# A decode block with adaLN, sliding-window attention and an MLP: the tile framework replaced by a recorder in the kernel, and another end of the program

## Chip, cores and metric

One Trainium2 chip, one of its cores. The metric is the device time of one execution in microseconds, the median of several runs. All times below are from the chip.

## What is computed

Two tokens (B = 2, one position each, D = 512) pass through one block. A vector `c` gives six modulation vectors through SiLU and one matrix. Attention reads the last W = 4096 positions of a cache of 32768, with 32 query heads over 8 key/value heads of width 128. The MLP has F = 1792 hidden units. Everything is fp32.

```python
mod = (_silu(c) @ w_mod).reshape(c.shape[0], 6, 1, -1)
sa, ca, ga, sb, cb, gb = (mod[:, i] for i in range(6))
h = _layernorm(x) * (1 + ca) + sa
q = (h @ wq) as 32 heads
p = softmax(q @ k_cache[:, :, Sk - W:].T * Dh ** -0.5)   # 4 query heads share a kv head
x = x + ga * ((p @ v_cache[:, :, Sk - W:]) @ wo)
h = _layernorm(x) * (1 + cb) + sb
x = x + gb * (_silu(h @ w1) @ w2)
```

The inputs that are read: w_mod 6.3 MB, wq 8.4 MB, the windows of both caches 67 MB, wo 8.4 MB, w1 and w2 3.7 MB each; 97.5 MB in all. The result is 4 KB.

## The kernel before

The kernel is written in a framework (a tile context). The kernel asks for tiles from pools and calls engine operations; the framework orders the instructions of each engine, except where `inorder` pins them, and puts in the semaphores. It closes the program on leaving the context (line 569, inside `kernel`): SyncE waits for all semaphores, the engines meet, GpSimd clears the semaphores, the engines meet again. Line 558 is the constructor of the program object; it writes some constants and lets the engines meet once at the start.

**Memory.** One tile `store` of 36,864 floats on each of 128 partitions holds four slots of 8,192 floats (4 MB each) and a spare part. w_mod first lies in the last third, over slot 3 and the spare part; wq lies in slots 0 and 1.

**Loads.** SyncE issues all big loads, in this order: w_mod (line 78), wq in two halves (86), then K and V of eight steps (line 93, in `load_cache`) in the order k0, k1, v0, k2, v1, ..., k7, v6, v7, one slot each in rotation; then wo in four pieces, w1 in three and w2 in five (line 405, in `load_rows`). Each load waits until the engines have read what lay in its slot. ACT issues two small loads, c and x (line 82). `fetch` decides how far ahead the program text issues loads.

**Start.** GpSimd makes an identity matrix, and DVE sums pieces of it into small selection matrices (lines 107 to 139). `moments` (182 to 200) takes mean and variance of x with two small matmuls and a Sqrt on ACT. `silu_exp` (174 to 177) gives SiLU of c through an Exp on ACT. Matmuls with w_mod (222) give `m_a` (the first two modulation vectors) and `m_b` (the other four); `h_a` (230) is the modulated input. Matmuls with wq (242) give q, which is spread into `qbd` (253 to 267).

**Attention.** `seq` has eight steps: four pairs of kv heads, two tokens. A step t has three parts. `scores(t)` (287 to 322): four DVE transposes of the K slot, each followed by matmuls with `qbd`; then the row maximum, its spread over the partitions through two matmuls, and an Exp with row sums on ACT. `probabilities(t)` (327 to 345) turns the result for the next product. `values(t - 1)` (355 to 365): 16 matmuls over the V slot and, for the second token of a pair, four that collect `o_all`. The loop runs scores(t), values(t - 1), probabilities(t); these instructions are pinned in this order.

**End.** The sums of the softmax (`lp`, 424) are inverted and give the normalised output `oTn` (443). `product` and `narrow` (456) are the matmuls with wo, w1 and w2, some over 512 columns and some over 128. `fill` (451) issues matmuls that nobody reads. After wo come the residual, the second LayerNorm (482 to 506), w1, SiLU, and w2: products 0 to 7 into `yw`, copied by ACT (466) and folded by a matmul with `id4` into `y`, into which the last six products go as w2's last pieces land. DVE multiplies by gb and adds the residual (542, 543), and SyncE stores (545).

Of the kernel before, what the change touches and what calls it, by code (L numbers as in the profile page):

```python
# [1 line left out]

# [6 lines left out]
F32 = mybir.dt.float32  # L9
AF = mybir.ActivationFunctionType  # L10
ALU = mybir.AluOpType
AX = mybir.AxisListType

P = 128
# [11 lines left out]
@with_exitstack  # L26
def adaln_block(
    ctx: ExitStack,
    tc: tile.TileContext,
    x: bass.AP,  # L30
    k_cache: bass.AP,
    v_cache: bass.AP,
    wq: bass.AP,
    wo: bass.AP,
    w1: bass.AP,
    w2: bass.AP,
    c: bass.AP,
    w_mod: bass.AP,
    out: bass.AP,
):  # L40
# [6 lines left out]
    nc = tc.nc  # L47
# [6 lines left out]
    big = ctx.enter_context(tc.tile_pool(name="big", bufs=1))  # L54
    store = big.tile([P, 36864], F32, name="store")
    slot = [store[:, i * SLOT : (i + 1) * SLOT] for i in range(4)]
    consts = ctx.enter_context(tc.tile_pool(name="consts", bufs=1))
    ktp = ctx.enter_context(tc.tile_pool(name="ktp", bufs=3))
    work = ctx.enter_context(tc.tile_pool(name="work", bufs=2))
    once = ctx.enter_context(tc.tile_pool(name="once", bufs=1))  # L60
    psum = ctx.enter_context(tc.tile_pool(name="psum", bufs=2, space=bass.MemoryType.PSUM))
    psum1 = ctx.enter_context(tc.tile_pool(name="psum1", bufs=1, space=bass.MemoryType.PSUM))
    inorder = tc.keep_in_program_order

    def const(shape, name):
        return consts.tile(shape, F32, name=name)

    def bank(tag, name):
        return (psum1 if tag in "CO" else psum).tile([P, 512], F32, tag=tag, name=name)
# [4 lines left out]
    for t in (c_sp, x_sp):  # L74
        nc.vector.memset(t, 0.0)
    rows8 = lambda t: t.rearrange("(ab r) m -> ab r m", r=16)[:, 0, :]
    wm = store[:, 24576:36864].rearrange("p (k e) -> p k e", k=4)
    nc.sync.dma_start(
        wm.rearrange("p k e -> p (k e)"), w_mod.rearrange("(p k) e -> p (k e)", k=4)
    )  # L80
    for t, src in ((c_sp, c), (x_sp, x2)):
        nc.scalar.dma_start(rows8(t), src.rearrange("b (g m) -> g b m", m=P))
    wqt = store[:, :16384].rearrange("p (k e) -> p k e", k=4)
    wq4 = wq.rearrange("(p k) e -> p (k e)", k=4)
    for i in range(2):
        nc.sync.dma_start(slot[i], wq4[:, i * SLOT : (i + 1) * SLOT])
# [4 lines left out]
    def load_cache(cache, t, where):  # L91
        hp, b = seq[t]
        nc.sync.dma_start(
            where,
            cache[b, 2 * hp : 2 * hp + 2, SK - W :, :].rearrange(
                "u (i n) d -> i u (n d)", n=NK
            ),
        )
        return where
# [3 lines left out]
    make_identity(nc, ident)  # L103

    def summed(shape, name, pattern, axis=AX.X, **sizes):
        t = const(shape, name)
        nc.vector.tensor_reduce(t, ident.rearrange(pattern, **sizes), axis=axis, op=ALU.add)
        return t
# [3 lines left out]
    nc.vector.tensor_scalar(  # L112
# [3 lines left out]
    nc.vector.tensor_copy(  # L116
# [6 lines left out]
    nc.vector.tensor_reduce(  # L123
# [7 lines left out]
    nc.vector.tensor_reduce(  # L131
# [7 lines left out]
    nc.vector.tensor_reduce(  # L139
# [5 lines left out]
    for i in range(1, 4):  # L145
        nc.gpsimd.tensor_copy(pick[:, :, :, i], pick[:, :, :, 0])
        nc.gpsimd.tensor_copy(sums[:, :, :, i], sums[:, :, :, 0])
# [3 lines left out]
    nc.gpsimd.memset(mean512, 1.0 / D)  # L151
    negscale = const([1, 1], "negscale")
    nc.vector.memset(negscale, -SCALE)
    eps_t = const([P, 1], "eps_t")
    nc.vector.memset(eps_t, EPS)
    mrow = [const([1, P], f"mrow{i}") for i in range(2)]
    for t in mrow:
        nc.gpsimd.memset(t, 0.0)
    qbd = [const([P, 4, B, 4, 32], f"qbd{n}") for n in range(2)]
    qg = [const([P, 4, B, 4, G], f"qg{n}") for n in range(2)]  # L160
    for t in qg + qbd:
        nc.gpsimd.memset(t, 0.0)
    rowsum = const([P, NP], "rowsum")
    oTn = const([P, 32, 32], "oTn")
    nc.gpsimd.memset(oTn, 0.0)
# [3 lines left out]
    nc.gpsimd.memset(hT, 0.0)  # L169
    nc.gpsimd.memset(uT, 0.0)  # L170

    def silu_exp(t, name, shape):
        e = once.tile(shape, F32, tag="silu", name=name)
        nc.vector.tensor_scalar(e, t, -1.0, 87.0, op0=ALU.mult, op1=ALU.min)
        nc.scalar.activation(e, e, AF.Exp)
        nc.vector.tensor_scalar(e, e, 1.0, None, op0=ALU.add)
        nc.vector.reciprocal(e, e)
        return e

    def moments(t, name):  # L180
        st = work.tile([P, 6], F32, tag="st6", name=f"st_{name}")
        nc.vector.bn_stats(st, t)
        mv = work.tile([P, 2], F32, tag="mv", name=f"mv_{name}")
        nc.vector.bn_aggr(mv, st)
        avgm = avg.rearrange("p a r -> p (a r)")
        sm = bank("B", f"mean_{name}")
        nc.tensor.matmul(sm[:, 0:1], avgm, mv[:, 0:1], start=True, stop=True)  # L187
        mean = work.tile([P, 1], F32, tag="mean", name=f"m_{name}")
        nc.vector.tensor_copy(mean, sm[:, 0:1])
        dm = work.tile([P, 2], F32, tag="dm", name=f"dm_{name}")  # L190
        nc.vector.tensor_sub(dm[:, 0:1], mv[:, 0:1], mean)
        nc.vector.scalar_tensor_tensor(
            dm[:, 1:2], dm[:, 0:1], dm[:, 0:1], mv[:, 1:2], op0=ALU.mult, op1=ALU.add
        )
        sv = bank("B", f"var_{name}")
        nc.tensor.matmul(sv[:, 0:1], avgm, dm[:, 1:2], start=True, stop=True)
        std = work.tile([P, 1], F32, tag="std", name=f"sd_{name}")
        nc.scalar.activation(std, sv[:, 0:1], AF.Sqrt, bias=eps_t)
        rstd = work.tile([P, 1], F32, tag="rstd", name=f"rs_{name}")
        nc.vector.reciprocal(rstd, std)  # L200
        return mean, rstd

    def turned(t, name):
        o = const([P, 4, 32], name)
        nc.vector.transpose(o, t.rearrange("p (m k) -> p k m", k=4))
        return o
# [3 lines left out]
    xn = once.tile([P, P], F32, tag="xs", name="xn_a")  # L210
    nc.vector.tensor_scalar(xn, x_sp, mean_a, rstd_a, op0=ALU.subtract, op1=ALU.mult)
# [3 lines left out]
    nc.vector.tensor_mul(scT, cT, sg)  # L215
    m_a = bank("A", "m_a")[:, : 2 * P]
    m_b = bank("D", "m_b")
    for s0, s1, m in ((0, 2, m_a), (2, 6, m_b)):
        for k in range(4):
            v = wm[:, k].rearrange("p (s g m) -> p g s m", s=6, g=4)  # L220
            for g in range(4):
                nc.tensor.matmul(
# [6 lines left out]
    h_a = once.tile([P, P], F32, tag="h", name="h_a")  # L229
    nc.vector.scalar_tensor_tensor(h_a, m_a[:, P:], 1.0, xn, op0=ALU.add, op1=ALU.mult)  # L230
    nc.vector.tensor_add(h_a, h_a, m_a[:, :P])
    hq_T = turned(h_a, "hq_T")
    nc.scalar.copy(mod_sp[:, 2:, :].rearrange("p s m -> p (s m)"), m_b)
    nc.gpsimd.tensor_scalar(mod_sp[:, 4, :], mod_sp[:, 4, :], 1.0, None, op0=ALU.add)
    ga, sb, cb1, gb = (mod_sp[:, s, :] for s in range(2, 6))

    q_ps = [bank("D", f"q{n}") for n in range(2)]
    for k in range(4):
        for n in range(2):
            wv = wqt[:, k].rearrange("p (n s g m) -> p n g s m", n=2, s=4, g=G)  # L240
            for g in range(G):
                nc.tensor.matmul(  # L242
# [6 lines left out]
    for n in range(2):  # L249
        qT = once.tile([P, D], F32, tag="wide", name=f"qT{n}").rearrange(  # L250
            "p (s j r) -> p s j r", s=4, r=32
        )
        nc.vector.transpose(qT.rearrange("p s j r -> p (s j r)"), q_ps[n])  # L253
        for g in range(G):
            r = slice(32 * g, 32 * g + 32)
            eng = nc.gpsimd if g % 2 else nc.vector
# [3 lines left out]
        rp = bank("C", f"qr{n}")[:, :P]  # L260
        nc.tensor.matmul(
            rp, rep4, qg[n].rearrange("p s b j g -> p (s b j g)"), start=True, stop=True
        )
        for i in range(4):
            r = slice(32 * i, 32 * i + 32)
            cp = nc.scalar.copy if i % 2 else nc.vector.tensor_copy
# [12 lines left out]
    o_all = bank("O", "o_all")[:, : B * DH].rearrange("p (b d) -> p b d", b=B)  # L279

    def scores(t):
        hp, b = seq[t]
        s_ps = bank("A", f"s{t}")
        kv = kt[t].rearrange("p (n j r) -> p n j r", n=NK, j=4)
        for j in range(4):
            kT = ktp.tile([P, NK, 32], F32, tag="kT", name=f"kT{t}")
            inorder(nc.vector.transpose(kT, kv[:, :, j, :]))  # L287
            for u in range(2):
                h = 2 * hp + u
                for f in range(2):  # L290
                    r = 32 * (2 * u + f)
                    inorder(nc.tensor.matmul(  # L292
# [5 lines left out]
                    ))  # L298
        mx = work.tile([P, 1], F32, tag="mx", name=f"mx{t}")
        inorder(nc.vector.tensor_reduce(mx, s_ps, axis=AX.X, op=ALU.max))  # L300
        mT = bank("B", f"mT{t}")
        inorder(nc.tensor.matmul(mT[0:1, :P], mx, ident, start=True, stop=True))  # L302
        mg = work.tile([1, 2, G], F32, tag="mg", name=f"mg{t}")
        inorder(nc.vector.tensor_reduce(
# [6 lines left out]
        ))  # L311
        m = mrow[t % 2]
        for u in range(2):
            inorder(nc.vector.tensor_copy(  # L314
                m.rearrange("o (u f v a g) -> o u f v a g", u=2, f=2, v=2, g=G)[:, u, :, 0],
                mg[:, u, None, None, :].to_broadcast([1, 2, 4, G]),
            ))
        bp = bank("B", f"bp{t}")
        inorder(nc.tensor.matmul(bp[:, 0:1], m, negscale, start=True, stop=True))  # L319
        bias = work.tile([P, 1], F32, tag="bias", name=f"bias{t}")  # L320
        inorder(nc.scalar.copy(bias, bp[:, 0:1]))  # L321
        inorder(nc.scalar.activation(  # L322
            pr, s_ps, AF.Exp, bias=bias, scale=SCALE, accum_out=rowsum[:, t : t + 1]
        ))

    def probabilities(t):
        inorder(nc.vector.transpose(xp, pr))  # L327
        for f in range(2):
            inorder(nc.vector.tensor_mul(  # L329
# [3 lines left out]
            ))  # L333
        tp = bank("C", f"pT{t}")[:, : 4 * NK]
        for a in range(4):
            inorder(nc.tensor.matmul(  # L336
# [5 lines left out]
            ))  # L342
        pt = ptb[t % 2].rearrange("p (n u g) -> p n u g", u=2, g=G)
        for u in range(2):
            inorder(nc.scalar.activation(  # L345
                pt[:, :, u, :], tp.rearrange("p (n g) -> p n g", g=G), AF.Copy,
                scale=par[:, u : u + 1],
            ))

    def values(t):  # L350
        hp, b = seq[t]
        o_ps = bank("D", f"o{t}")
        for i in range(16):
            c_ = i % 4
            inorder(nc.tensor.matmul(  # L355
# [5 lines left out]
            ))  # L361
        inorder(nc.scalar.copy(ob[:, b].rearrange("p n d -> p (n d)"), o_ps))  # L362
        if b == B - 1:
            for n in range(4):
                inorder(nc.tensor.matmul(  # L365
# [6 lines left out]
                ))  # L372
# [29 lines left out]
    def load_rows(w, per, lo, hi, s, at):  # L402
        e = w.shape[1]
        n = (hi - lo) * e
        nc.sync.dma_start(s[:, at : at + n], w.rearrange("(p q) e -> p (q e)", q=per)[:, lo * e : hi * e])
# [13 lines left out]
    nc.vector.tensor_copy(hT[:, :, 1:32:16], sbT[:, :, 0:32:16])  # L419


    lp = bank("B", "lp")
    for hp in range(HP):
        nc.tensor.matmul(
# [6 lines left out]
    rl = once.tile([P, B], F32, tag="rl", name="rl")  # L431
    nc.vector.reciprocal(rl, lp[:, :B])
    rq = once.tile([P, B, 4], F32, tag="rq", name="rq")
    nc.vector.tensor_mul(
# [138 lines left out]
```

## Time and profile before

| | |
|---|---|
| median of 3 runs | 237.02 us (236.94 to 237.02) |
| the profiled execution | 237.04 us |
| its span, first to last instruction | 235.2 us |
| mean granted clock of TensorE | 0.832 |
| PE, DVE, ACT, POOL busy | 147.3, 113.2, 28.8, 7.1 us |
| moved by DMA | 97.68 MB, 415 GB/s over the span |

In profile lines PE is TensorE's matmul, PEld its weight load, DVE VectorE, ACT ScalarE, POOL GpSimd and SP SyncE; a "q" behind an engine (SPq) marks what its sequencer does: DMA issues, semaphore waits, drains. A timeline row has start, duration (both us), engine, line, operation, output <- inputs, shape and count; in square brackets, how long the engine stood idle before and what ended that. A row of stretches has the bounds, the length, the busy time of PE, PEld, DVE, ACT and POOL with instruction counts, TensorE's granted clock, the share of time in which the 16 DMA engines were busy, and GB/s. A row of DMA issues has the count, the size of each and the median time from issue to landing. A row of waits has the total, the number of waits and the longest. "instruction" queues carry the engines' own instructions.

### The profile page before, as it was taken

What the parts mean: (1) busy time and instruction counts of PE and PEld (TensorE: products, weight loads), DVE (VectorE), ACT (ScalarE), POOL (GpSimd) and SP (SyncE); (2) the same over time, 40 slices, a digit from 0 to 9 for tenths busy, and PEclk for the clock granted to TensorE, in tenths of its full rate; (3) what the DMA queues carried; (4) which work ended last, traced back from release to release, by engine and by line L of the source; (5) the groups of instructions that cost most, each with busy time, mean ns of one, the idle gap of its engine ahead of it and who ended that gap; (6) DMA issues with size and microseconds to landing.
All of it is one profiled execution on the core that took longest, in us unless ns stands there. A gap on an engine that the chain in (4) does not pass through costs nothing.

```text
span 235.2 us, 2446 instructions
## 1 busy us (share of the span) xinstructions
PE 147.3 (63%) x1024; PEld 39.8 (17%) x1024; DVE 113.2 (48%) x155; ACT 28.8 (12%) x64; POOL 7.1 (3%) x27
## 2 busy tenths in 40 slices
PE   0005953738258866887865838818757597677973
PEld 0003311110010211232101300200211132224212
DVE  0126110478397695894395387459439430102030
ACT  2010000010310120211200110210120102012210
POOL 5004000100000000000000000000000000000000
PEclk9999996756956797797679985976995759999799
DMA  7999999999999999999999999999999999999991
GB/s 267 461 432 429 418 426 418 446 440 446 425 429 412 426 446 435 440 426 418 423 440 429 437 440 423 423 429 437 435 430 429 429 426 440 401 415 418 421 400 41
DMA packets 4510, 97.68 MB, mean 415 GB/s; under 512 B 508, under 2 KB 532, under 8 KB 1044
## 3 DMA queue, kind: packets, MB, share of 16 engines
q1 hardware_dynamic: 4476, 97.52, 97.1%
q8 instruction: 8, 0.13, 0.2%
q14 instruction: 2, 0.02, 0.0%
q10 hardware_dynamic: 24, 0.01, 0.0%
HBM read 97.53 MB, written 0.00 MB: 415 GB/s over the span
## 4 chain that ended last, share of the span: by engine, by line
DMA 61%; DVE 23%; issue 6%; PE 6%; ACT 2%; SPq 0%; POOL 0%; POOLq 0%
DMA store<-in_A_k_cache_dram 25%; DVE kT L287 17%; DMA store<-in_A_wq_dram 16%; DMA store<-in_A_wo_dram 11%; DMA store<-in_B_w_dram 9%; PE q L242 2%; PE s L292 2%; DVE store L329 2%; ACT store L322 1%; DVE store L327 1%; DVE mx L300 1%; PE acc_y L456 1%; DVE qT L253 1%; ACT L322 1%; PE bp L319 1%
## 5 line engine op out<-in xcount | busy, mean ns | idle before, releaser
L287 DVE STREAM_TRANSPOSE kT<-store 128x2048 f32<-128x2048 f32 x32 | 71.1, 2280 | 15.8 <-DMA store<-in_A_k_cache_dram 15.7
L292 PE MATMUL s<-kT,qbd 128*32 128x512 f32 x256 | 49.5, 857 | 28.5 <-DVE kT L287 28.5
L355 PE MATMUL o<-store 128*32 128x512 f32 x256 | 38.2, 749 | 1.0 <-ACT store L345 1.0
L292 PEld LDWEIGHTS s<-kT,qbd 128*32 128x32 f32 x256 | 6.3, 126 | 66.4 <-DVE kT L287 65.7
L242 PE MATMUL q<-store,hq_T 128*32 128x512 f32 x64 | 9.7, 759 | 6.1 <-DMA store<-in_A_wq_dram 6.1
L355 PEld LDWEIGHTS o<-store 128*32 128x32 f32 x256 | 9.5, 132 | 22.4 <-issue 20.8
L187 PE MATMUL mean_a<-mv_a,avg 128*128 128x1 f32 x2 | 0.6, 362 | 18.8 <-DVE avg L112 18.8
L327 DVE STREAM_TRANSPOSE store<-store 128x512 f32<-128x512 f32 x8 | 5.7, 712 | 13.6 <-ACT store L322 13.6
L321 ACT COPY bias<-bp 128x1 f32<-128x1 f32 x8 | 1.3, 159 | 87.7 <-PE bp L319 87.7
L300 DVE TENSOR_REDUCE mx<-s 128x1 f32<-128x512 f32 x8 | 5.5, 692 | 11.0 <-PE s L292 11.0
L329 DVE TENSOR_TENSOR store<-store,half 128x512 f32<-128x512 f32 x16 | 10.4, 688 | 0.2
L336 PE MATMUL pT<-store,sel 128*32 128x256 f32 x64 | 7.5, 414 | 4.5 <-DVE store L329 4.5
L365 PE MATMUL o_all<-store,pick 128*32 128x256 f32 x32 | 7.7, 382 | 2.9 <-ACT store L362 2.9
L362 ACT COPY store<-o 128x512 f32<-128x512 f32 x8 | 4.7, 586 | 32.4 <-PE o L355 32.4
L345 ACT ACTIVATE store<-pT,par 128x256 f32<-128x256 f32 x16 | 6.7, 476 | 10.8 <-PE pT L336 10.8
L253 DVE STREAM_TRANSPOSE qT<-q 128x512 f32<-128x512 f32 x2 | 1.4, 717 | 13.3 <-PE q L242 13.0
L456 PE MATMUL acc_o<-store,oTn 128*32 128x512 f32 x48 | 5.6, 595 | 3.0 <-DMA store<-in_A_wo_dram 3.0
L302 PE MATMUL mT<-ident,mx 128*1 128x128 f32 x16 | 3.0, 271 | 6.5 <-DVE mx L300 6.5
L319 PE MATMUL bp<-negscale,mrow 1*128 1x1 f32 x16 | 3.2, 265 | 5.1 <-DVE mrow L314 5.1
L438 DVE TENSOR_TENSOR on<-o_all,rq 128x256 f32<-128x256 f32 x1 | 0.4, 425 | 12.2 <-PE o_all L365 12.2
L482 DVE STREAM_TRANSPOSE aoT<-ao 128x128 f32<-128x128 f32 x1 | 0.3, 317 | 11.6 <-PE ao L456 11.6
L451 PE MATMUL unread<-qbd,mean 128*128 128x256 f32 (+2 forms) x12 | 5.8, 566 | 0.1
(123 smaller groups left out, 93.4 us busy)
## 6 DMA issues: line engine op xcount, KB each, us to landing
store<-in_A_k_cache_dram SPq DMA_DIRECT2D x8, 4096.0 KB, 29.9
store<-in_A_v_cache_dram SPq DMA_DIRECT2D x8, 4096.0 KB, 29.8
store<-in_A_wq_dram SPq DMA_DIRECT2D x2, 4096.0 KB, 31.8
store<-in_w_mod_dram SPq DMA_DIRECT2D x1, 6144.0 KB, 17.2
store<-in_A_wo_dram SPq DMA_DIRECT2D x1, 4096.0 KB, 32.6
store<-in_B_w_dram SPq DMA_DIRECT2D x3, 1024.0 KB, 23.4
store<-in_A_wo_dram SPq DMA_DIRECT2D x1, 2048.0 KB, 25.1
store<-in_A_wo_dram SPq DMA_DIRECT2D x2, 1024.0 KB, 28.2
```

What stands on the lines that cost most here:

```text
L242: nc.tensor.matmul(q_ps[n][32 * g : 32 * g + 32, :], hq_T[:, k, :], wv[:, n, g], start=(k == 0), stop=(k == 3),)
L287: inorder(nc.vector.transpose(kT, kv[:, :, j, :]))
L292: inorder(nc.tensor.matmul(s_ps[r : r + 32, :], qbd[h // 4][:, h % 4, b, j, :], kT[:, 32 * f : 32 * f + 32, u:32:2], start=(j == 0), stop= ...
L300: inorder(nc.vector.tensor_reduce(mx, s_ps, axis=AX.X, op=ALU.max))
L327: inorder(nc.vector.transpose(xp, pr))
L329: inorder(nc.vector.tensor_mul(zp[:, 32 * f : 32 * f + 32, :].rearrange("p (s y) w -> p s y w", y=2), xp[:, :, None, 0:16].to_broadcast([P ...
L336: inorder(nc.tensor.matmul(tp[32 * a : 32 * a + 32, :], sel, zp[:, :, 4 * a : 4 * a + 4], start=True, stop=True,))
L345: inorder(nc.scalar.activation(pt[:, :, u, :], tp.rearrange("p (n g) -> p n g", g=G), AF.Copy, scale=par[:, u : u + 1],))
L355: inorder(nc.tensor.matmul(o_ps[32 * c_ : 32 * c_ + 32, :], ptb[t % 2][:, 32 * i : 32 * i + 32], vt[t][:, 512 * i : 512 * i + 512], start= ...
L365: inorder(nc.tensor.matmul(o_all[32 * hp : 32 * hp + 32, :, :], pick[:, n].rearrange("p w i -> p (w i)"), ob[:, :, n, :], start=(n == 0), ...
L451: inorder(nc.tensor.matmul(bank("C", "unread")[:, :n], mean512, idle_w[:, :n], start=True, stop=True))
L456: inorder(nc.tensor.matmul(acc[32 * g : 32 * g + 32, :n], w, rows, start=start, stop=stop))
```

## The change

The framework goes. `Flow` stands in its place: `fl.dve.tensor_mul(...)` and the like are recorded, not issued. For each operation `record` takes the region that it reads or writes of each tensor (first and last partition, first and last element in a partition, a box around strided accesses) and notes which earlier operations it must follow. `emit` then issues everything in program order. An operation waits for another engine's operation only where nothing that its engine has already waited for covers it. An engine other than TensorE also waits for its own earlier writes where they are read or overwritten; GpSimd waits for all its own earlier operations. Each engine has one semaphore, each DMA one of its own (34 of them).

At the end, the framework's closing is gone. PE, DVE, ACT and SyncE each add one to `done`, SyncE behind the issue of the store. GpSimd waits for the four and clears all semaphores but the store's. SyncE waits for the store and clears that one.

Pools become plain buffers: three for the transposed K pieces in turn (`kts`), two `wide` ones, eight PSUM banks handed out in turn by tag as before, and a buffer of its own for each small tile. The calculation, the shapes, the loads and the store are those of before. The text of the kernel body changes in names alone (`nc.vector` becomes `dve`, `inorder(...)` goes), but its order now is the order of every engine: the constants at the top, then `moments` of x, then SiLU of c; `lp` behind the last `values`.

The diff, cut to its core:

```diff
-    big = ctx.enter_context(tc.tile_pool(name="big", bufs=1))
-    store = big.tile([P, 36864], F32, name="store")
+    store = buf("store", P, 36864)
...
+class Flow:
+    NAMES = {"pe": "tensor", "dve": "vector", "act": "scalar", "pool": "gpsimd", "sp": "sync"}
...
+    def record(self, engine, method, args, kw):
+        aps = [(k, v) for k, v in (*enumerate(args), *kw.items()) if isinstance(v, bass.AP)]
+        outs = {0, "out", "accum_out"} if 0 in dict(aps) else {"out", "accum_out"}
+        me = len(self.ops)
+        needs = set()
+        for writes in (False, True):
+            for k, ap in aps:
+                if (k in outs) != writes or "dram" in ap.tensor.name:
+                    continue
+                r = self.region(ap)
+                held = self.seen.setdefault(ap.tensor.name, [])
+                for other, w, o in held:
+                    if (w or writes) and other != me and (
+                        r[0] < o[1] and o[0] < r[1] and r[2] < o[3] and o[2] < r[3]
+                    ):
+                        needs.add((other, w))
...
+        if engine == "pool":
+            needs |= {(i, True) for i, o in enumerate(self.ops) if o[0] == "pool"}
+        self.ops.append((engine, method, args, kw, needs))
+
+    def emit(self):
...
+        for i, (engine, method, _, _, needs) in enumerate(ops):
+            mine, wait = known[engine], []
+            for d, wrote in sorted(needs, reverse=True):
+                p = proc[d]
+                if p == engine and (engine == "pe" or not wrote):
+                    continue
+                if mine.get(p, -1) >= d:
+                    continue
+                wait.append(d)
+                told.add(d)
...
+            for d in waits[i]:
+                eng.wait_ge(*value[d])
+            ins = getattr(eng, method)(*args, **kw)
+            if method == "dma_start":
+                last = nc.alloc_semaphore(f"dma{i}")
+                ins.then_inc(last, 16)
+                value[i] = (last, 16)
+            elif i in told:
+                count[engine] += 1
+                ins.then_inc(sems[engine], 1)
+                value[i] = (sems[engine], count[engine])
+
+        for e in ("pe", "dve", "act", "sp"):
+            getattr(nc, self.NAMES[e]).sem_inc(done, 1)
+        nc.gpsimd.wait_ge(done, 4)
+        first = min(s.num for s in sems.values())
+        nc.gpsimd.sem_clear(range(first, last.num))
+        nc.sync.wait_ge(last, 16)
+        nc.sync.sem_clear(last)
...
-            inorder(nc.vector.transpose(kT, kv[:, :, j, :]))
+            kT = kts[(4 * t + j) % 3]
+            dve.transpose(kT, kv[:, :, j, :])
...
+    fl.emit()
...
-    with _tile.TileContext(nc) as tc:
-        adaln_block(tc, *args)
+    adaln_block(nc, *args)
```

404 lines of the change are left out of this document (215 added, 189 removed).

## The prediction

> **What bounds the kernel now.** I read the page first, then the stretches of the span, then the timeline of both ends, the instructions of the line that closes the program, and the DMA queue's own waits. From the page:
>
> ```profile
> span 235.2 us, 2446 instructions
> ...
> q1 hardware_dynamic: 4476, 97.52, 97.1%
> q8 instruction: 8, 0.13, 0.2%
> ...
> DMA 61%; DVE 23%; issue 6%; PE 6%; ACT 2%; SPq 0%; POOL 0%; POOLq 0%
> ```
>
> Queue q1 carries 97.52 MB and keeps the 16 DMA engines 97.1% busy: 228 of 235.2 us. The last line, the chain that ended last, tempts one to see 23% of DVE work that could shrink. The stretches, whose last columns are the granted clock, the DMA share and GB/s, say otherwise:
>
> ```profile
> 2.00:60.00 58.00, 26.58 (x168) 7.43 (x168) 20.60 (x44) 4.75 (x9) 5.72 (x17) 0.85 0.98 422
> 60.00:228.00 168.00, 117.93 (x796) 30.98 (x800) 91.65 (x106) 23.45 (x54) 0.00 (x0) 0.82 1.00 428
> 229.00:230.00 1.00, 0.42 (x8) 0.16 (x8) 0.00 (x0) 0.34 (x1) 0.00 (x0) 1.00 0.54 207
> 230.00:231.00 1.00, 0.95 (x36) 0.95 (x40) 0.00 (x0) 0.00 (x0) 0.00 (x0) 1.00 0.30 109
> ```
>
> From 60 to 228 us no DMA engine rests; only then do they finish, one after the other. The kernel is a stream of fixed length with a head and a tail, and only the head, the tail and what thins the stream can move the time. The profiled execution took 237.04 us, its span 235.2, so 1.8 us lie outside the span. The median of the runs is 237.02: what holds for this execution holds for it to 0.02 us.
>
> **The tail: what goes.** First the last steps of the timeline, then the instructions of line 569 up to 234.52 us, then those of the whole line (columns: engine, operation, count, shortest, median and longest in ns, first and last start):
>
> ```profile
> 230.05 1.70 PE L456 MATMUL acc_y<-store,uT 128*32 128x128 f32 x48 [0.23 <-DMA store<-in_B_w_dram]
> 231.31 0.16 PEld L456 LDWEIGHTS acc_y<-store,uT 128*32 128x32 f32 x8 [0.24 <-DMA store<-in_B_w_dram]
> 231.81 0.29 DVE L542 TENSOR_TENSOR yo<-acc_y,mod_sp 128x128 f32<-128x128 f32 x1 [5.33 <-PE acc_y L456]
> 232.13 0.29 DVE L543 TENSOR_TENSOR yo<-yo,x 128x128 f32<-128x128 f32 x1
> 232.45 0.69 SPq L545 DMA_DIRECT2D out_dram<-yo  x1
> ```
>
> ```profile
> L569 SPq EVENT_SEMAPHORE  x5: 28/28/947, 233.3 to 234.4; - x5
> ```
>
> ```profile
> L569 POOLq EVENT_SEMAPHORE  x4: 17/17/17, 234.6 to 235.1; - x4
> ...
> L569 POOLq EVENT_SEMAPHORE_RANGE_CLEAR  x1: 96/96/96, 234.9 to 234.9; - x1
> ```
>
> The store is issued from 232.45 to 233.14. SyncE's first wait of these five, 0.947 us from 233.3 on, ends when the store has landed, at 234.2. The span ends at 235.2, so 1.0 us is pure closing: SyncE's four further waits to 234.5, a meeting of all engines (GpSimd's events from 234.6 on), the clear at 234.9, and a second meeting (its events to 235.1).
>
> The change keeps everything up to 234.2 and puts one clear of one semaphore on SyncE in place of the closing. No row shows a clear on SyncE. Its nearest bounds are 0.02 us, the shortest event instruction (0.017), and 0.22, GpSimd's clear of 0.096 with two separate instructions around it (0.06 each, as four waits fill 234.2 to 234.5). I take 0.1, the row of the same operation. So 1.0 - 0.1 = 0.9 us goes.
>
> Two waits are added there. GpSimd waits for four increments; the last is SyncE's, issued after the store at 233.14. Behind this wait stands only GpSimd's clear of some 39 semaphores (five engines', "done", and 33 of the 34 DMAs'), and nobody waits for it. At 0.096 us it ends near 233.3, so the store's landing hides it with 0.9 us to spare; without this cover it would cost its 0.1. SyncE's wait for the store has only the last clear behind it. The increments of PE, DVE and ACT come earlier, and nothing follows them.
>
> **The head: what moves.** The engines now run in program order. On DVE and ACT the LayerNorm of x stands before the SiLU of c, and the constants stand before both. DVE, then ACT, then PE before the change:
>
> ```profile
> 10.61 0.40 DVE L205 STREAM_TRANSPOSE cT<-c_sp 128x128 f32<-128x128 f32 x1 [9.41 <-DMA c_sp<-in_c_dram]
> 11.05 0.23 DVE L174 TENSOR_SCALAR sgc<-cT 128x128 f32<-128x128 f32 x1
> 16.05 0.29 DVE L182 BATCH_NORM_STATS2 st_a<-x_sp 128x6 f32<-128x128 f32 x1 [4.78 <-DMA x_sp<-in_A_x_dram]
> ...
> 18.05 0.36 DVE L107 TENSOR_REDUCE id<-ident 128x32 f32<-128x128 f32 x1
> ...
> 19.71 0.37 DVE L107 TENSOR_REDUCE quarter<-ident 128x4 f32<-128x128 f32 x1
> ```
>
> ```profile
> 11.31 0.31 ACT L175 ACTIVATE sgc<-sgc 128x128 f32<-128x128 f32 x1 [7.26 <-DVE sgc L174]
> 11.63 1.28 ACT L198 ACT_TABLE_LOAD   x1
> ```
>
> ```profile
> 21.30 3.64 PE L222 MATMUL m_a<-store,scT 128*32 128x256 f32 x32
> ```
>
> Before, c's transpose to its Exp (10.61 to 11.62, 1.0 us) hides ahead of x's landing at 16.05. Afterwards it waits in DVE's queue behind x's chain, with a table load (1.28) between Sqrt and Exp. In return the nine constants of 18.05 to 20.08 leave that path, 2.0 us, and fill the wait for c. So m_a moves from 21.30 by something between -2.0 and +2.3 us; I take +0.8, some 0.5 above the plain sum, since Sqrt's chain and c's now run one after the other. Behind it stand m_b and, on SyncE, the second K load, which overwrites part of w_mod:
>
> ```profile
> 28.52 0.54 SPq L93 DMA_DIRECT2D store<-in_A_k_cache_dram  x1
> ```
>
> ```profile
> 1.64 37.20 DMA store<-in_A_wq_dram
> ```
>
> At 28.52 the queue still holds the second half of wq, which lands at 38.84 (1.64 + 37.20), and behind it the first K load, 4.19 MB at 428 GB/s or 9.8 us more. The second K load may come 20 us later before a DMA engine starves: the head costs nothing, and with that cover gone one us for each us. GpSimd now also waits for each of its own writes; its 5.72 us of work in the first stretch may double and still be over before the q stage near 45.
>
> **The middle: waits that look like a prize.** Loads of w1 and w2 wait for loads of wo although they fill other slots: they reuse their semaphores. The change gives each DMA its own.
>
> ```profile
> SPq L405 <- DMA store<-in_A_wo_dram: 15.1, 4, 6.4
> ```
>
> ```profile
> store<-in_B_w_dram SPq DMA_DIRECT2D x3, 1024.0 KB, 23.4
> ```
>
> SyncE waits 15.1 us for that. But 1 MB takes 2.4 us to move and lands 23.4 us after its issue: for 21 us it stands in the queue. Issued earlier, it stands longer. For the same reason one table load fewer in the first softmax and waits for regions instead of tiles buy nothing: they bring issues forward, not landings.
>
> An added wait between engines costs up to 0.06 us (above). From 231.31 there are four handoffs, PE, DVE, DVE and SyncE: 0 to 0.24 us. A gain is excluded, as the steps follow each other within 0.03 us (231.81 + 0.29 to 232.13). I take 0, since each step has one releaser, for which the instruction itself can wait. Ahead of 231.31 PE idles 0.23 and 0.24 us for DMA, which absorbs a few more.
>
> Instruction fetch thins the stream. By its row each 16 KB packet of q8 holds one DMA engine 0.2% x 16 x 235.2 / 8 = 0.94 us, and the engines finish apart (share 0.54, then 0.30). One more packet on the engine that ends last would make the sum 0.9 worse. Eight packets stand against 2,446 instructions, one for 300; the change adds tens. I take 0, with 0.9 as the other end. The Trainium skill, "Runtime: NRT & Kernel Launch", section "Instruction fetch mechanics", calls crossing such a block mostly hidden; by that a ninth packet would be free, while the row shows a DMA engine held 0.94 us for each.
>
> Sum: 237.04 - 0.9 = 236.1 us. Its own range is 236.0 to 236.5 (clear 0.02 to 0.22, handoffs up to 0.24).
>
> **The rivals.** (1) The stream starts fuller. Between 2 and 60 us the DMA share is 0.98, which is 1.2 us of idle; with half of it recovered the time is 235.5. Against it: the first loads wait for nothing that the change touches. (2) The change does only half of what it says: the second meeting belongs to the program and not to the context, and stays. From 234.8 to 235.2 that is 0.4 us, so 236.5. Against it: both meetings carry line 569, the context's. (3) What the span loses comes back outside it, in the 1.8 us: 237.0. Nothing in the trace speaks for it or against it. The Trainium skill, same page, section "The ~15µs preamble/postamble breakdown", has the runtime wait for all engines after any kernel, about 1.5 us; by that the meeting outside is paid in both versions and 236.1 stands. No run here shows that meeting. (4) Slower: PE's clock halves in the closing matmuls, because the sums of the softmax (line 424) now come after the last value product, and the moved head shifts PE's load. The same eight matmuls at two clocks, and the closing stretch:
>
> ```profile
> 181.67 1.94 PE L292 MATMUL s<-kT,qbd 128*32 128x512 f32 x8 [0.26 <-DVE kT L287]
> 183.86 1.10 PE L292 MATMUL s<-kT,qbd 128*32 128x512 f32 x8 [0.26 <-DVE kT L287]
> ```
>
> ```profile
> 177.20:183.60 6.40, 5.80 (x24) 0.61 (x24) 6.40 (x4) 0.00 (x0) 0.00 (x0) 0.50 1.02 440
> 183.80:185.00 1.20, 1.10 (x8) 0.16 (x8) 0.01 (x1) 0.00 (x0) 0.00 (x0) 1.00 1.02 437
> 226.50:231.80 5.30, 4.21 (x72) 1.66 (x72) 0.00 (x0) 0.59 (x1) 0.00 (x0) 1.00 0.62 246
> ```
>
> They take 1.94 us at granted clock 0.50 and 1.10 at 1.00, 1.76 times as long. The closing 4.21 us of PE would become 7.4, 3.2 more; PE's two idle pieces absorb 0.5, so 236.1 + 2.7 = 238.8. It decides once more than 0.9 us is lost there. Against it: the clock in the closing stretch is 1.00, and PE's order there, filler matmuls included, stays.
>
> **How the numbers follow.** The forecast gets 0.70, (1) 0.08, (2) 0.07, (3) 0.08, (4) 0.07. A measurement of this kernel tells 0.2%, 0.47 us, from no change, so faster means under 236.55. Rival (2) lies at that edge and is halved: faster 0.70 + 0.08 + 0.03 = 0.81, same 0.08 + 0.04 = 0.12, slower 0.07. The range 235.4 to 236.8 holds the forecast with both ends of its bounds, (1) and (2), 0.85 in all, and leaves out (3) and (4).
>
> **What would show it.** Right: a DMA share of 1.00 from 60 to 228 us and eight packets on q8; late weights issued earlier that land when they did; the last matmuls near 231.3 and the store near 232.5; SyncE's last wait ending near 234.2 with the span 0.1 behind it; GpSimd's clear near 233.3; m_a near 22. Wrong: a store over 0.3 us away from 232.5, a meeting of the engines at the end, another time outside the span than 1.8 us, or a granted clock well under 1.00 after 226.

## The result, and the profile after

The median went from 236.98 us (6 runs beside it, 236.85 to 237.05) to 235.55 us (6 runs, 235.49 to 235.99): a ratio of 0.9943, 95% interval 0.9931 to 0.9956. The profiled execution of the changed kernel took 235.64 us, that of the kernel before 237.04, so 1.40 us went between these two. They divide as follows. The span went from 235.25 to 234.32 us, which is 0.93 less, and the time outside the span from 1.79 to 1.32, which is 0.47 less.

First the page of the kernel after, with its span, two queues, the chain that ended last and the row of three late weight loads:

```profile
span 234.3 us, 2365 instructions
...
q1 hardware_dynamic: 4476, 97.52, 97.4%
q8 instruction: 8, 0.13, 0.2%
...
DMA 68%; DVE 23%; PE 6%; ACT 1%; issue 1%; POOL 0%; SPq 0%
...
store<-in_B_w_dram SPq DMA_DIRECT2D x3, 1024.0 KB, 31.1
```

Fewer instructions, not more (2,365 against 2,446), in the same eight packets. "issue" in the chain fell from 6% to 1%, and not a microsecond of the result is there: the late loads now need 31.1 us from issue to landing where they needed 23.4. They are issued earlier (the last at 206.62 us instead of 213.97, the third last even at 197.37 instead of 208.99) and land when they did (the last at 231.35, before at 231.27; the third last at 230.10, before at 230.00). The stretches say the same; columns as before:

```profile
2.00:60.00 58.00, 25.68 (x169) 7.16 (x170) 19.15 (x40) 4.75 (x9) 7.38 (x21) 0.88 0.98 422
60.00:228.00 168.00, 114.42 (x796) 29.88 (x798) 93.36 (x110) 23.04 (x53) 0.00 (x0) 0.85 1.00 428
229.00:230.00 1.00, 0.43 (x8) 0.16 (x8) 0.00 (x0) 0.36 (x1) 0.00 (x0) 1.00 0.56 217
230.00:231.00 1.00, 0.86 (x32) 0.86 (x36) 0.00 (x0) 0.00 (x0) 0.00 (x0) 1.00 0.31 119
226.50:231.80 5.30, 3.97 (x72) 1.50 (x64) 0.00 (x0) 0.59 (x1) 0.00 (x0) 1.00 0.65 255
```

DMA share 0.98 in the head, 1.00 from 60 to 228 us, and 428 GB/s, as before. The last steps of the timeline:

```profile
230.14 1.68 PE L114 MATMUL bankD<-store,uT 128*32 128x128 f32 x48 [0.30 <-DMA store<-in_B_w_dram]
231.40 0.16 PEld L114 LDWEIGHTS bankD<-store,uT 128*32 128x32 f32 x8 [0.23 <-DMA store<-in_B_w_dram]
231.89 0.29 DVE L114 TENSOR_TENSOR yo<-bankD,mod_sp 128x128 f32<-128x128 f32 x1 [5.69 <-PE bankD L114]
232.22 0.29 DVE L114 TENSOR_TENSOR yo<-yo,x 128x128 f32<-128x128 f32 x1
232.54 0.70 SPq L114 DMA_DIRECT2D out_dram<-yo  x1
```

Each step is 0.08 or 0.09 us later than before, the amount by which the last weights landed later. The difference begins behind the store. Two answers for the two lines that clear (engine, operation, count, shortest, median and longest in ns, first and last start):

```profile
L128 POOLq EVENT_SEMAPHORE_RANGE_CLEAR  x1: 247/247/247, 233.3 to 233.3; - x1
```

```profile
L130 SPq EVENT_SEMAPHORE_RANGE_CLEAR  x1: 30/30/30, 234.3 to 234.3; - x1
```

The store has landed at 234.27. SyncE's clear of one semaphore takes 0.030 us and is the last instruction of the program, from 234.29 to 234.32. GpSimd is done at 233.58, PE, ACT and DVE at 231.8, 229.4 and 232.5. In the kernel before, the second meeting let all five engines go within 0.1 us of 235.2.

### The profile page after: what moved, and what is told of

The parts are those of the page before. It is cut to its first block, busy times and chain, and to the rows that moved or that the text cites. A ratio compares the mean times of both kernels' runs of the same rounds, so it can differ in the third digit from the quotient of the medians.

```text
span 234.3 us, 2365 instructions
## 1 busy us (share of the span) xinstructions
PE 142.9 (61%) x1024; PEld 38.4 (16%) x1024; DVE 113.9 (49%) x155; ACT 28.4 (12%) x63; POOL 8.1 (3%) x27
## 4 chain that ended last, share of the span: by engine, by line
DMA 68%; DVE 23%; PE 6%; ACT 1%; issue 1%; POOL 0%; SPq 0%
DMA store<-in_A_k_cache_dram 25%; DVE kT L114 19%; DMA store<-in_A_wq_dram 16%; DMA store<-in_B_w_dram 14%; DMA store<-in_A_v_cache_dram 13%; PE bankD L114 4%; DVE store L114 2%; PE bankA L114 1%; ACT store L114 1%; PE bankB L114 1%; DVE wide L114 1%; DVE mx L114 1%; DVE qbd L114 0%; POOL qg L114 0%; PE bankC L114 0%
## 5 line engine op out<-in xcount | busy, mean ns | idle before, releaser
L114 PE MATMUL bankA<-kT,qbd 128*32 128x512 f32 x256 | 47.7, 825 | 31.8 <-DVE kT L114 31.8
L114 PE MATMUL bankD<-store 128*32 128x512 f32 x256 | 36.2, 716 | 1.7 <-DMA store<-in_A_v_cache_dram 1.7
L114 PEld LDWEIGHTS bankA<-kT,qbd 128*32 128x32 f32 x256 | 5.7, 122 | 69.1 <-DVE kT L114 69.1
L114 PE MATMUL bankD<-store,hq_T 128*32 128x512 f32 x64 | 9.5, 746 | 5.9 <-DMA store<-in_A_wq_dram 5.9
L114 PEld LDWEIGHTS bankD<-store 128*32 128x32 f32 x256 | 8.8, 129 | 22.4 <-issue 20.1
L114 DVE TENSOR_REDUCE mx<-bankA 128x1 f32<-128x512 f32 x8 | 5.5, 692 | 10.7 <-PE bankA L114 10.7
L114 PE MATMUL bankO<-store,pick 128*32 128x256 f32 x32 | 7.7, 382 | 2.9 <-ACT store L114 2.9
L114 PE MATMUL bankC<-store,sel 128*32 128x256 f32 x64 | 7.4, 414 | 3.1 <-DVE store L114 3.1
L114 ACT ACTIVATE store<-bankC,par 128x256 f32<-128x256 f32 x16 | 7.6, 476 | 10.9 <-PE bankC L114 10.7
L114 PE MATMUL bankD<-store,oTn 128*32 128x512 f32 x48 | 6.8, 729 | 3.4 <-DMA store<-in_A_wo_dram 3.4
## 6 DMA issues: line engine op xcount, KB each, us to landing
store<-in_B_w_dram SPq DMA_DIRECT2D x3, 1024.0 KB, 31.1
```

The costliest lines, as they stand in the source:

```text
L114: ins = getattr(eng, method)(*args, **kw)
```

## The experiments

The part within the span was forecast. What had to be found is where the other 0.5 us came from, and whether the terms that the prediction set to zero really are zero. The theories on the 0.5 us: it belongs to the form of the end (the program no longer makes its engines leave together); or, the rival that the expectations call B, to the framework's program as a whole, whatever its end. Two finer forms of the first came up on the way. One says that the time outside is about 1.8 us whenever any engine besides SyncE is held to the end (M in the expectations); the other, that each engine has a length of its own from its last instruction to the end of the measured time, and the latest sum of the two sets the time (L).

The table has all runs that bear on this. "Outside" is the time less the span, the median over the runs with the lowest and highest; the spans of single runs are known to 0.1 us. It holds what passes before the first instruction as well as what passes after the last, and no run splits the two. As these kernels differ at their ends, the runs show how the part behind the last instruction changes, and not how long it is by itself; a "length" below includes the same share from before the first instruction. close2 to pool_last ran on one chip, hold_act to fetch on another, c_first to late_k1 on a third, beside runs of the kernel before with medians of 236.98, 237.03 and 236.98 us; its row in the table has the outside of the first of these.

| kernel | held to the end | median us | ratio, 95% interval | outside, us |
|---|---|---|---|---|
| before | all five | 236.98 | | 1.84 (1.78 to 1.93) |
| after | SyncE | 235.55 | 0.9943, 0.9931 to 0.9956 | 1.34 (1.29 to 1.39) |
| close2 | all five | 236.75 | 0.9990, 0.9981 to 0.9999 | 1.82 (1.74 to 1.92) |
| meet | all five | 236.25 | 0.9968, 0.9956 to 0.9980 | 1.81 (1.77 to 1.92) |
| hold_pe | SyncE, PE | 235.80 | 0.9953, 0.9941 to 0.9966 | 1.65 (1.60 to 1.71) |
| pool_last | GpSimd | 236.07 | 0.9960, 0.9948 to 0.9973 | 1.87 (1.83 to 1.90) |
| hold_act | SyncE, ACT | 235.77 | 0.9947, 0.9935 to 0.9960 | 1.47 (1.45 to 1.57) |
| hold_dve | SyncE, DVE | 235.83 | 0.9947, 0.9934 to 0.9961 | 1.45 (1.41 to 1.54) |
| clear_late | SyncE | 235.70 | 0.9942, 0.9930 to 0.9955 | 1.36 (1.29 to 1.42) |
| fetch | SyncE | 235.68 | 0.9943, 0.9930 to 0.9955 | 1.37 (1.33 to 1.41) |
| c_first | SyncE | 235.46 | 0.9935, 0.9918 to 0.9951 | 1.41 (1.36 to 1.43) |
| eight | SyncE | 235.51 | 0.9938, 0.9923 to 0.9953 | 1.34 (1.32 to 1.39) |
| fetch2 | SyncE | 244.05 | 1.0295, 1.0271 to 1.0319 | 1.31 (1.28 to 1.37) |
| late_k1 | SyncE | 242.25 | 1.0222, 1.0202 to 1.0243 | 1.40 (1.33 to 1.46) |

### The recorder with a closing like the framework's (close2)

```diff
-        for e in ("pe", "dve", "act", "sp"):
-            getattr(nc, self.NAMES[e]).sem_inc(done, 1)
-        nc.gpsimd.wait_ge(done, 4)
+        for s, n in [(sems[e], count[e]) for e in ("pe", "dve", "act", "pool")] + [(last, 16)]:
+            nc.sync.wait_ge(s, n)
+        nc.all_engine_barrier()
         first = min(s.num for s in sems.values())
-        nc.gpsimd.sem_clear(range(first, last.num))
-        nc.sync.wait_ge(last, 16)
-        nc.sync.sem_clear(last)
+        nc.gpsimd.sem_clear(range(first, last.num + 1))
+        nc.all_engine_barrier()
```

> The recorder with the framework's closing: SyncE waits for every engine and the store, two meetings of all engines, GpSimd's clear of all semaphores between them. Theory L (each engine needs time of its own after its last instruction, and the slowest engine's is 0.5 us longer than SyncE's): span 235.3, 1.8 us outside, 237.1 us, the time of before. Theory B (0.5 us outside belongs to the framework's program, whatever its end): span 235.3, 1.3 outside, 236.6. If the recorder itself gains in the stream, it is below both.

236.75 us, 0.23 below the kernel before and 1.2 above the kernel after; outside 1.82. The second meeting in its trace:

```profile
L129 POOLq EVENT_SEMAPHORE  x2: 17/17/17, 234.8 to 234.8; - x2
...
L129 SPq EVENT_SEMAPHORE  x1: 17/17/17, 234.9 to 234.9; - x1
...
L129 PEldq EVENT_SEMAPHORE  x1: 51/51/51, 234.9 to 234.9; - x1
```

The same closing in the kernel before has these events up to 235.2: its SyncE waits four more times behind the store's landing (234.2 to 234.5), here there is next to nothing between the landing and the meeting. From the store's landing to the end of the span pass 0.83 us here and 1.05 there, and that is the 0.23 us, of the closing again. The median of 236.75 lies nearer to B's 236.6 than to L's 237.1, because both forecasts had a span of 235.3 and it is 235.0. What tells them apart is the time outside: with both meetings put back, nothing is left of the gain there, so B falls. 61 instructions fewer, the earlier issues and the regions are worth nothing that can be measured.

### One meeting, one engine held, another engine last (meet, hold_pe, pool_last)

`meet` puts one meeting of all engines behind SyncE's clear. `hold_pe` holds PE alone. `pool_last` lets SyncE go after the issue of the store, and GpSimd waits for it and clears.

```diff
         nc.sync.sem_clear(last)
+        nc.all_engine_barrier()
```

> The changed kernel with one meeting of all engines after SyncE's last clear. Span 234.3 + 0.45 = 234.8. Theory L: 1.8 outside, 236.6 us. Theory B: 1.3 outside, 236.1.

```diff
         nc.sync.sem_clear(last)
+        go = nc.alloc_semaphore("go")
+        nc.sync.sem_inc(go, 1)
+        nc.tensor.wait_ge(go, 1)
+        nc.tensor.sem_clear(go)
```

> The changed kernel, but PE alone stays until the store has landed (SyncE tells it, PE clears that semaphore). Span 234.5. Theory L, if PE is the engine with the long leg: 1.8 outside, 236.3 us; if not, at most SyncE's 1.3, 235.8 or less. Theory B: 235.8.

```diff
-        nc.sync.wait_ge(last, 16)
-        nc.sync.sem_clear(last)
+        nc.gpsimd.wait_ge(last, 16)
+        nc.gpsimd.sem_clear(last)
```

> The changed kernel, but SyncE leaves after issuing the store, and GpSimd waits for the store and clears its semaphore. Span 234.3 to 234.4. Theory L: the time outside becomes GpSimd's own leg, anything from 0.8 to 1.8, so 235.1 to 236.2 us. Theory B: 1.3 outside, 235.7.

`meet` costs 0.7 us, of which only 0.25 lie in its span (it ends at 234.57, with SyncE's clear at 234.3): the rest is 1.81 us outside instead of 1.34. The expectation had 0.45 us for the meeting, so the median lies nearer to B's 236.1 than to L's 236.6, though the time outside is L's 1.8. `pool_last` is the telling one, since it has no meeting and no instruction more than the kernel after. Its page, and then the answer for its last line:

```profile
span 234.1 us, 2365 instructions
```

```profile
L130 POOLq EVENT_SEMAPHORE_RANGE_CLEAR  x1: 44/44/44, 234.0 to 234.0; - x1
```

Its span is 0.2 us shorter than the kernel's after, and it takes 0.5 us longer: with GpSimd's clear as the last instruction 1.87 us lie outside the span, with SyncE's 1.34. So it isn't the meeting as such that costs outside the span, but which engine leaves late. With PE held it is 1.65 us. The median of hold_pe, 235.80, is what B forecast, but only because its span came out some 0.3 us shorter than the 234.5 of both theories; its time outside is not B's 1.3.

### The other two engines held (hold_act, hold_dve)

The edit is that of hold_pe, with `nc.scalar` and `nc.vector` in place of `nc.tensor`.

> The changed kernel, but ACT alone stays until the store has landed, told by SyncE. Span 234.3 to 234.4 in every theory. Theory L, by the legs so far (time outside the span: SyncE last 1.3, PE last 1.7, GpSimd last 1.8): ACT is an engine like PE, its leg 1.6 to 1.8, 236.0 us. Theory M (the runtime's work after the kernel is 1.8 us long whenever more than SyncE is left): 1.8, 236.1. If ACT's leg is under 1.2 the time stays at SyncE's 235.6.

> The same with DVE alone held until the store has landed. Theory L: DVE has its own leg, between 1.3 and 1.8: 235.6 to 236.1 us, and not the same as PE's or ACT's to 0.1. Theory M: 1.8 outside, 236.1.

1.47 and 1.45 us outside, well short of 1.8: M falls, L stands. Two of L's own forecasts missed all the same: ACT is not like PE (1.6 to 1.8 expected), and DVE and ACT do not differ from each other by 0.1. By the runs the lengths are SyncE 1.34, DVE 1.45, ACT 1.47, PE 1.65, GpSimd 1.87 us. SyncE's is between 1.31 and 1.41 in the medians of the seven kernels that hold it alone, so DVE's and ACT's are hardly longer and their ranges overlap with it; PE's and GpSimd's stand apart from these and from each other.

L can be tested on the profiled executions. After: SyncE leaves at 234.32, plus 1.34 is 235.66; GpSimd leaves at 233.58, plus 1.87 is 235.45; measured 235.64. That is no test, as SyncE's 1.34 comes from the runs of this kernel. The other three are, as GpSimd's 1.87 comes from pool_last. Before: GpSimd's last event ends at 235.16, plus 1.87 is 237.03; measured 237.04. close2: 234.86 plus 1.87 is 236.73; measured 236.74. meet: 234.48 plus 1.87 is 236.35; measured 236.44, so 0.1 is missing there. The change of 1.40 is then 0.84 for an engine that leaves earlier and 0.53 for another engine that leaves last.

The Trainium skill, "Runtime: NRT & Kernel Launch", section "The ~15µs preamble/postamble breakdown", has the runtime wait for all engines behind a kernel, at about 1.5 us. That the last one decides agrees with these runs; one figure for all of them does not, with 1.34 to 1.87 us by engine. No trace here shows what an engine does in this time.

### All clears after the store (clear_late)

No meeting, but SyncE waits for the others and the store, and clears all 40 semaphores at the end: only the clear beside the store is undone.

```diff
-        for e in ("pe", "dve", "act", "sp"):
+        for e in ("pe", "dve", "act", "pool"):
             getattr(nc, self.NAMES[e]).sem_inc(done, 1)
-        nc.gpsimd.wait_ge(done, 4)
+        nc.sync.wait_ge(done, 4)
         first = min(s.num for s in sems.values())
-        nc.gpsimd.sem_clear(range(first, last.num))
         nc.sync.wait_ge(last, 16)
-        nc.sync.sem_clear(last)
+        nc.sync.sem_clear(range(first, last.num + 1))
```

> The changed kernel, but all 40 semaphores are cleared by SyncE after the store has landed, with no meeting. The clear of one took 0.030 us on SyncE, of 39 on GpSimd 0.247. If clearing beside the store is worth what that row says: span +0.2, time +0.2, 235.75 to 235.8. If SyncE's leg outside the span runs on regardless, the same. If the hiding is worth nothing: 235.55.

```profile
L129 SPq EVENT_SEMAPHORE_RANGE_CLEAR  x1: 99/99/99, 234.0 to 234.0; - x1
```

SyncE clears 40 in 0.099 us, where one takes it 0.030. By these rows the clear beside the store saves 0.07 us. From the store's landing to the end of the span pass 0.17 us here and 0.05 in the kernel after, so 0.12 with the wait. The median is 0.15 above that of the kernel after, with ranges that overlap (235.50 to 235.82 against 235.49 to 235.99), but only 0.02 above that of `fetch`, which ran on the same chip and turned out to be a repeat of the kernel after (below). No more than 0.15 can be said. Nearly all of the gain is in what no longer stands behind the store's landing, waits and meetings, and in the engine that leaves last; next to none is in clearing while the store runs.

### The head and the semaphores (c_first, eight)

`c_first` puts the SiLU of c ahead of the LayerNorm of x again. `eight` lets each DMA wait for the eighth before it, as if semaphores were reused.

```diff
-    mean_a, rstd_a = moments(x_sp, "a")
-    xn = buf("xn_a", P, P)
...
     dve.tensor_mul(scT, cT, sg)
+    mean_a, rstd_a = moments(x_sp, "a")
+    xn = buf("xn_a", P, P)
```

> The changed kernel with the SiLU of c ahead of the LayerNorm of x in program order. m_a starts about 2 us earlier, near 20, and so does the second K load, near 27. If the stream binds: 235.55 to 235.7, no difference. If the head counts: up to 2 us less.

```diff
+            if method == "dma_start" and len(loads) >= 8:
+                eng.wait_ge(*value[loads[-8]])
...
+                loads.append(i)
```

> The changed kernel, but each DMA is issued only when the eighth DMA before it has landed, as the framework's eight semaphores had it. The last loads of w2 are issued up to 10 us later. If the queue only grows longer by an early issue: 235.55 to 235.7, landings as before. If loads that stand ready sooner help the stream: slower, up to 0.5 us.

In c_first m_a starts at 18.25 instead of 22.12, the second K load is issued 4.6 us earlier (24.18 instead of 28.77) and lands at 58.00 instead of 58.36; the time is 235.46 (235.36 to 235.63), 0.09 under the kernel after, with ranges that overlap, and 0.05 under eight, which ran beside it. The expectation had m_a only 2 us earlier, and not 3.9. In eight SyncE's waits for wo are back:

```profile
SPq L115 <- DMA store<-in_A_wo_dram: 16.8, 4, 8.1
```

16.8 us of waits (15.1 in the kernel before), and 235.51 us (235.35 to 235.63). Both are zero within the spread of the runs, as the prediction had them.

### The cover taken away (late_k1)

The head was called free because the queue holds 20 us of work when the second K load is issued. Here this load, and all behind it, waits for DVE's first transpose of the first K slot; only one more load is asked for at that place.

```diff
+        if engine == "sp" and self.held_by is not None:
+            needs.add((self.held_by, True))
+            self.held_by = None
...
+            if t == 0 and j == 0:
+                fl.held_by = len(fl.ops) - 1
...
-    fetch(4)
+    fetch(1)
```

> The changed kernel, but the second K load, and with it every later load, waits for the first transpose of the first K tile, which ends near 51.4 us. The first K load has landed at 46.6 to 48.7, and data flows about 1.0 us after an issue, so the engines stand idle for 3.7 us (the last) to 5.8 (the first). If the queue's content is the cover: 239.3 to 240.8 us. If compute had slack of its own to give back, or the rate could catch up: under 238.

242.25 us, 6.7 more than the kernel after. Three stretches of late_k1, then the same of the kernel after:

```profile
40.00:48.00 8.00, 5.38 (x32) 1.48 (x24) 2.74 (x8) 0.52 (x2) 0.98 (x4) 0.79 0.75 324
48.00:54.00 6.00, 2.75 (x14) 0.41 (x17) 5.73 (x5) 0.52 (x2) 0.00 (x0) 0.68 0.29 87
54.00:60.00 6.00, 4.50 (x26) 0.45 (x18) 4.42 (x3) 0.00 (x0) 0.00 (x0) 0.75 1.01 437
```

```profile
40.00:48.00 8.00, 5.37 (x35) 1.31 (x26) 2.74 (x8) 0.52 (x2) 0.98 (x4) 0.79 1.05 455
48.00:54.00 6.00, 2.75 (x14) 0.61 (x18) 5.53 (x5) 0.52 (x2) 0.00 (x0) 0.69 1.00 431
54.00:60.00 6.00, 4.43 (x25) 0.45 (x18) 4.62 (x3) 0.00 (x0) 0.00 (x0) 0.74 0.99 426
```

The DMA engines rest for 0.25 of 8 us and 0.71 of 6 us, 6.3 us in all, and nothing makes up for it. The same late weight load in both chains that ended last, late_k1 first:

```profile
203.98 32.75 DMA store<-in_B_w_dram
```

```profile
197.37 32.73 DMA store<-in_B_w_dram
```

It lands 6.6 us later (236.73 against 230.10). The expectation that the stream would catch up falls. The one for one loss stands, but was priced some 1.5 us low. One part is the restart: the load issued at 51.17 into an empty queue has landed at 63.49, 12.3 us later, where one in the stream follows the one before it by 9.7. Of these 2.6 us the expectation had 1.0. The other part is that the engines, once in step again (landings within 0.32 us of each other instead of 2.07), are out of step again by 1.84 us two loads later; in these two loads the lag behind the kernel after grows from 5.1 to 6.6 us.

### One instruction packet more (fetch, fetch2)

The other end of the bound on instruction fetch was 0.9 us for a ninth packet.

```diff
+        for _ in range(260):
+            nc.tensor.nop()
```

> The changed kernel with 260 empty instructions at the start of PE's stream, which end before its first matmul at 16.7, so that one more 16 KB packet of instructions is fetched (9 on q8). If each packet goes to another DMA engine: the latest engine is the same, 235.55 to 235.65 us. If the ninth lands on the latest engine, as the prediction priced it: +0.9, and by the skew of the landings +1.5, so 236.5 to 237.1.

This tells nothing of packets: the empty instructions did not reach the program, which again has 2,365 instructions and eight packets. 235.68 us is a repeat of the kernel after.

```diff
+        spare = nc.alloc_semaphore("spare")
+        for _ in range(260):
+            nc.tensor.sem_inc(spare, 1)
```

> The changed kernel with 260 semaphore increments at the start of PE's stream, 0.05 us each, over by 14 us, before PE's first matmul at 16.7. One more packet on q8 (9). If each packet goes to another DMA engine: 235.55 to 235.75 us. If it lands on the engine that ends last: 0.9 us more by the prediction's price, 1.5 by the spread of the landings, so 236.5 to 237.1.

244.05 us, 8.5 more than the kernel after, and again not a price of fetch, though it has the ninth packet. Its packets, the added instructions, PE's first matmul and two stretches:

```profile
q8 instruction: 9, 0.15, 0.2%
```

```profile
L111 PEldq EVENT_SEMAPHORE  x260: 51/51/51, 0.8 to 40.7; - x130
```

```profile
40.77 0.56 PE L117 MATMUL bankB<-mv_a,avg 128*128 128x1 f32 x2 [40.77 <-issue]
...
53.05 0.54 SPq L117 DMA_DIRECT2D store<-in_A_k_cache_dram  x1
```

```profile
40.00:48.00 8.00, 2.99 (x24) 1.93 (x28) 3.06 (x10) 1.85 (x3) 0.00 (x0) 1.00 0.75 324
48.00:54.00 6.00, 6.00 (x56) 1.89 (x52) 0.99 (x3) 0.08 (x1) 0.00 (x0) 1.00 0.00 0
```

An increment has a row of 0.051 us, but 260 of them take 40 us, 0.154 each. They hold PE's first matmul to 40.77, the second K load is issued at 53.05, when the queue has been empty for 5 us, and it lands 8.4 us late. That is the whole loss, a second and harder case of late_k1. In both runs it is the time for which the queue was empty, from the landing of the first K load to the next issue, and 3.6 to 3.9 us more: 2.85 of 6.7 us in late_k1 (48.32 to 51.17), 4.86 of 8.5 here (48.19 to 53.05). The last weights land within 1.93 us of each other (1.91 in the kernel after), so by this spread the ninth packet did not hold the DMA engine that ends last, and the 0.9 us did not fall due. What it costs where it does is not shown.

## Why the prediction was right, and which step failed

**The closing.** 1.0 us less a clear of 0.1, 0.9 in sum. Measured 0.93 within the span. SyncE's clear took 0.030 us, near the lower bound of 0.02 and not the 0.1 that was taken.

**GpSimd's clear.** Forecast 0.096 us, ending near 233.3. It took 0.247 and ended at 233.58. It is hidden as the prediction said, but the cover isn't the 0.9 us left until the store lands: with GpSimd's 1.87 us outside, where SyncE has 1.34, it leaves 0.2 us (235.45 against 235.66).

**The time outside the span: the step that failed.** The sum 237.04 - 0.9 carries the 1.8 us outside the span over unchanged, without a row that speaks for it, and another value stands among the signs that would prove the prediction wrong. It is 1.32 in the profiled execution. The runs show why: GpSimd, with a length of 1.87, was held to the end before, and now SyncE with 1.34 leaves last. The only alternative considered was that it grows (rival 3); that it shrinks, because another engine leaves last, was in none of the cases. So the time lies 0.45 below the forecast's own range of 236.0 to 236.5. It lies within the wide range only because that reached down to 235.4, to take in rival 1 at 235.5, a fuller start, which did not happen: 0.98 of DMA share in the head, as before. That is luck. The sum was right in its sign and in its largest term, and short by a third.

**The head.** m_a near 22: 22.12, but two errors cancel in it. With c first again m_a is at 18.25, so the rest of the change brings it forward by 3.05 us where the prediction had 2.0 for the constants, and the new order delays it by 3.87 where it had 2.8. No cost: c_first takes the 3.87 us back for nothing that can be told from the spread. The condition, the cover of 20 us, is shown by late_k1 and fetch2, which take it away and lose 6.7 and 8.5 us.

**The middle.** Zero, as said: late loads issued earlier landing as before, and eight puts the waits back for nothing.

**Handoffs and packets.** The store is issued 0.09 us later than before, 0.08 of it from the last landing; the handoffs cost 0. Eight packets, as said, though the instructions became 81 fewer, where the prediction had some tens more.

**The rivals.** (2), a second meeting that stays, did not come: behind the store's issue stand only SyncE's increment, the waits of GpSimd and SyncE and the two clears. (3), a loss outside the span, went the other way. (4), PE's clock in the closing, did not come: 1.00 granted from 226.5 to 231.8, with PE busy for 3.97 us.

Of all versions run, none is clearly faster than the changed kernel: c_first (235.46) and eight (235.51) have ranges that overlap with its own.

## What to carry to other kernels

In these runs the time ends a fixed length after an engine's last instruction, this length differs by engine, and the latest sum counts, so the end of a span isn't the end of the time: let the engine with the short tail (here SyncE) do the last wait, let the others leave as soon as they have nothing to do, and do not make all engines meet at the end. Treat the time outside the span as a term with a price of its own whenever an edit changes which engine leaves last. In a kernel that streams without rest, earlier issues are worth nothing while the queue holds work, and each microsecond of an empty queue is lost whole, plus the restart (3.6 to 3.9 us here).

## What the runs showed of the hardware

- The measured time exceeds the span by 1.34 us where SyncE is the last engine, by 1.45 with DVE, 1.47 with ACT, 1.65 with PE and 1.87 with GpSimd. SyncE, DVE and ACT can hardly be told apart (SyncE's medians run from 1.31 to 1.41). How much of it lies before the first instruction, and what happens in it, stays open.
- Clearing semaphores: one takes 0.030 us on SyncE, 0.041 on ACT, 0.044 on GpSimd, 0.055 on DVE, 0.063 on PE; 40 take 0.099 on SyncE, and 39 take 0.247 on GpSimd.
- 260 semaphore increments in a row on PE start 0.154 us apart, three times the 0.051 us of their rows.
- An instruction packet puts the 16 DMA engines out of step. In the kernel after, the landings of the first half of wq lie within 0.61 us, those of the second half within 2.06: 15 engines still within 0.60 of the first, and one 1.5 us later, after a 16 KB packet at 34.5 us that held it for 1.0 us and slowed its next packet by 0.5 (1.72 us instead of 1.21). The spread stays near 2.1 until the stream ends, though seven more packets follow. The Trainium skill, "Runtime: NRT & Kernel Launch", section "Instruction fetch mechanics", calls crossing such a block mostly hidden; for the engine that executes that may hold, but this trace shows 1.5 us taken from one DMA engine.
